# The MLP of an attention, convolution-gate and mixing kernel in five blocks of 924 tokens and one pass over its weights

## The chip, the cores and the metric

One core of a Trainium2 chip runs the whole program. The metric is device time in microseconds (us) from launch to end. Three runs of the kernel before took 1380.43 to 1383.66 us, median 1380.76.

Its engines run side by side, each through its own instructions in order: PE (TensorE) multiplies matrices into the accumulators (PSUM, eight banks of 512 floats per partition), DVE (VectorE), ACT (ScalarE) and POOL (GpSimd) work element by element, and SP (SyncE) issues the transfers between DRAM and on-chip memory.

## The reference, cut to what matters

Three stages follow each other on 8 sequences of 576 tokens (4608 in all). Only the last one, and its preparation, is touched here.

```
x  = attention(q, k, v, w_phi)                      # linear attention, 8 heads of 64
x  = (sigmoid(causal conv of x) * (x @ w_val)) @ w_out
u  = x + real(fft2(x))                              # over the sequence and the 512 features
un = (u - mean(u)) / sqrt(var(u) + 1e-6)            # over the 512 features: "LN"
y  = u + relu(un @ w_ch1) @ w_ch2                   # 512 -> 2048 -> 512: "MLP"
```

## The kernel before, in words

Every product is done in three matmuls on operands split into a high and a low part (high x high, high x low, low x high). A split is two instructions: `o_hi` (a rounding copy on ACT) and `o_lo` (a subtraction on DVE or POOL).

**The MLP's products.** Both layers use Strassen's scheme for 2x2 blocks in Winograd's form: seven products of sums of blocks instead of eight. The two halves of a block's tokens are one side of the 2x2, so a matmul is as wide as half a block. The sums of the weights' quarters are made once, in the mixing (`note_sums`, L375), and lie in DRAM (`w_scr`): eight pieces of 128 columns for each of 8 parts `j` of the 2048 hidden features, of both layers.

**Blocks and passes.** Nine blocks of `TB` = 512 tokens (L25), so matmuls of `HB` = 256 columns. The split weights of half the hidden features fill on-chip memory, so there are two passes over the blocks (`blocks`, L542): in the first, parts 0 to 3, the partial sums go to DRAM (`part_scr`) and the normed block to `un_scr`; in the second, parts 4 to 7, both come back. `prep_w` (L662) loads raw weight sums, 448 KB at a time, and splits them: three parts in the mixing's end, the others in the first block and at the turn between the passes (`note_mlp`, L1072). `prep_un` (L770) makes the seven operands out of a normed block by four subtractions and seven splits, for each of the 18 block passes.

**Units.** `c1_units` (L799) is the first layer of a pair of parts: seven products of 12 matmuls, into banks x, y and z, with copies, sums, relus and splits between them (13 or 14 DVE instructions and 14 of ACT). x has two banks, which the units take in turn. The results are the `h` tiles. `c2_units` (L874) is the second layer: seven products of 12 matmuls into cx, cy and cz, each then added to `acc`, which begins as u and leaves as the output. The second layer of a pair runs between the products of the next pair's first layer.

**LN.** `ln_stages` (L713) sums over features by DVE or POOL additions and a matmul with ones, into a bank of its own (mean). For block 0 it runs in the mixing, for the others in the MLP's first pass.

**What sets the order.** From the mixing on, all instructions are noted as operations with what they read and write, and `place_ops` (L1112) puts them in an order by planned durations and due times. It also chooses DVE or POOL for those marked "vp". On the chip each engine, and SP's queue of transfers, keeps that order, and each instruction waits for what it reads and for the place that it writes. There are stages, by which pools are open: at the mixing's end `open_last` and `open_mlp` (L564) open the tiles of the first layer, and in the last stage `open_mlp2` (L588) puts `h`, second-layer weights and `acc` where the mixing's tiles lay (among them `u`, the mixing's result on its way to DRAM).

In the profile nearly every instruction of these stages has line L62, that of the helper that issues it (L657 for transfers), so tiles tell them apart: x, y, z, cx, cy, cz are banks, un and h operands, w, wo and wg weights, A the block in LN, T scratch.

Of the kernel before, what the change touches and what calls it, by code (L numbers as in the profile page):

```python
# [20 lines left out]
NT = NB * S  # L21
# [3 lines left out]
TB = 512  # L25
HB = TB // 2
NBK = NT // TB
# [38 lines left out]
def attention_moe_mixer_kernel(  # L66
# [93 lines left out]
    un_scr = [dram.tile([128, 4, TB], F32, name=f"un_scr{t}") for t in range(NBK)]  # L160
# [3 lines left out]
    keep = pool(ctx, "keep", 1)  # L164
    wo_all = keep.tile([128, 2, 4 * DM], F32R, name="wo")
    wo = [wo_all[:, i].rearrange("p (c f) -> p c f", f=DM) for i in range(2)]
    P = {"g1": pool(ctx, "g1", 1)}

    mix = ExitStack()
# [22 lines left out]
    late["s1"] = ln_p.tile([128, TB], F32, name="s1")  # L192
    late["A"] = ln_p.tile([128, 4, TB], F32, name="A")
# [234 lines left out]
    def open_mix2():  # L428
# [3 lines left out]
        late["u"] = x2.tile([128, 4, S], F32, name="u")  # L432
        late["u256"] = x2.tile([97, S], F32, name="u256")
# [3 lines left out]
        for i in range(2):  # L437
            late["f", i] = x2.tile([128, 2, 2, NE], F32R, name=f"f{i}")
            late["Y", i] = x2.tile([128, 2, 2, NL], F32R, name=f"Y{i}")
            late["xr", i] = x2.tile([128, NE], F32R, name=f"xr{i}")  # L440
            late["rem", i] = x2.tile([128, NL], F32R, name=f"rem{i}")
            late["T0", i] = x2.tile([128, 2, HB], F32, name=f"T0{i}")
            late[("sh0", "sl0")[i]] = x2.tile([128, HB], F32R, name=("sh0", "sl0")[i])
        for i in range(4):
            late["ps", i] = ps.tile([128, 512], F32, name=f"ps{i}")
# [100 lines left out]
    NJP = NJ // 2  # L546
    NH_SLOTS = 7
    blocks = [(0, t) for t in range(NBK)] + [(1, t) for t in reversed(range(NBK))]
    wt = [[], []]
    wr = []  # L550
    un_op = []
    hs = []
    h_more = []
# [4 lines left out]
    def w_tiles(p, i, j):  # L558
        return [[p.tile([128, 7, 128], F32R, name=f"w{i}_{j}_{o}_{k}") for k in range(2)] for o in range(2)]

    def w_views(t):
        return [t[:, 896 * k:896 * k + 896].rearrange("p (q f) -> p q f", f=128) for k in range(2)]

    def open_mlp():  # L564
        p = pool(lx, "lx", 1, side=R)
        ps = pool(lx, "pss", 1, PSUM, side=R)
        late["mean"] = ps.tile([128, HB], F32, name="mean")
        for n in ("x0", "y"):
            late[n] = ps.tile([128, 2, HB], F32, name=n)
        for j in range(2):  # L570
            late["w", 0, j] = w_tiles(p, 0, j)
        for n in ("c11", "c12", "c22"):
            late[n] = p.tile([128, 2, HB], F32, name=n)
        for n in ("sh", "sl"):
            late[n] = p.tile([128, HB], F32R, name=n)
        for i in range(2):
            late["T", i] = p.tile([128, 2, HB], F32, name=f"T{i}")
            late["wr", i] = p.tile([128, 7, 128], F32, name=f"wr{i}")
# [3 lines left out]
        g = [P["g1"].tile([128, 2304], F32R, tag=f"g{i}", name=f"wg{i}") for i in range(2)]  # L582
        late["w", 0, 2] = [w_views(t) for t in g]
        late["w", 0, 3] = [w_views(wo_all[:, i]) for i in range(2)]
        h_more.extend(t[:, 1792:2304].rearrange("p (o f) -> p o f", f=HB) for t in g)
        h_more.append(wo_all[:, :, 1792:2048])

    def open_mlp2():  # L588
        big = pool(ctx, "big", 1)
        ps = pool(ctx, "psb", 1, PSUM)  # L590
        for n in ("x1", "z", "cx", "cy", "cz"):
            late[n] = ps.tile([128, 2, HB], F32, name=n)
        for i in range(NH_SLOTS):
            for k in range(2):
                late["h", i, k] = big.tile([128, 2, HB], F32R, name=f"h{i}_{k}") if 2 * i + k < 2 * NH_SLOTS - 3 else h_more.pop()
        for j in range(NJP):
            late["w", 1, j] = w_tiles(big, 1, j)
        for q in range(4):
            late["acc", q] = big.tile([128, 2, HB], F32, name=f"acc{q}")

    def late_tiles():
        for n in ("c11", "c12", "c22", "x0", "x1", "y", "z", "cx", "cy", "cz", "s1", "A", "sh", "sl", "mean", "u", "u256", "fs", ("T", 0), ("T", 1)):
            tl[n] = later(n)
        wr.extend(later(("wr", i)) for i in range(2))
        un_op.extend([later(("un", i, k)) for k in range(2)] for i in range(7))
        hs.extend([later(("h", i, k)) for k in range(2)] for i in range(NH_SLOTS))
        for i in range(2):
            for j in range(NJP):
                wt[i].append([[later(("w", i, j), o, k) for k in range(2)] for o in range(2)])
        for q in range(4):  # L610
            tl["acc", q] = later(("acc", q))

# [4 lines left out]
    BANKS = {"x0", "x1", "y", "z", "cx", "cy", "cz", "mean", "ps", "pv", "pa", "nm"}  # L617
    STAGES = {k: (a, b) for a, b, n in (
# [3 lines left out]
    ) for k in n.split()}  # L622

    def stage(k):
        n = k if isinstance(k, str) else k[0]
        if n in ("w", "ge"):
# [33 lines left out]
    wcount = [0]  # L660

    def prep_w(i, j, e):  # L662
        for o in range(2):
            b = wcount[0] % 2
            wcount[0] += 1
            h, l = wt[i][j % NJP][o]
            raw = wr[b]
            r = raw.rearrange("p q f -> p (q f)")
            wk = [("w", i, j % NJP, o, k) for k in range(2)]
            o_dma([(r, w_scr[i][j, o, :, 128:1024])], [("w_scr", i, j, o)], [("wr", b)], 448)  # L670
            was = {2: [("ge", 1, m, k) for m in range(4) for k in range(2)], 3: ["wo"]}.get(j, []) if i == 0 else []
            o_hi(h, raw, 896, [("wr", b)], [wk[0]] + was)
            o_lo(e, l, raw, h, 896, [("wr", b), wk[0]], [wk[1]] + was)
            yield
# [9 lines left out]
    AK = [("A", i, j) for i in range(2) for j in range(2)]  # L684

    def load_a(t, src):
        a = tl["A"]
        if src is un_scr:
            o_dma([(a, src[t])], [("un_scr", t)], AK, 1024)
            return  # L690
        parts = list(segments(t * TB, TB))
        o_dma([(a[:, :, o:o + n], src[b][:, :, s:s + n].rearrange("c p s -> p c s")) for o, n, b, s in parts],
              [("u_scr", b) for o, n, b, s in parts], AK, 1024)

    def load_acc(ps, t, q, after=[]):
        a = tl["acc", q]
        if ps:
            o_dma([(a, part_scr[t][q])], [("part", t, q)], [("acc", q)], 256)
            return
        i, j = divmod(q, 2)  # L700
        o_dma([(a[:, :, o:o + n], u_scr[b][2 * i:2 * i + 2, :, s:s + n].rearrange("c p s -> p c s"))
               for o, n, b, s in segments(t * TB + j * HB, HB)],
              after + [("u_scr", b) for o, n, b, s in segments(t * TB + j * HB, HB)], [("acc", q)], 256)

    def store_acc(ps, t, q):
        if ps == 0:
            o_dma([(part_scr[t][q], tl["acc", q])], [("acc", q)], [("part", t, q)], 256)
            return
        i, j = divmod(q, 2)
        o = t * TB + j * HB  # L710
        o_dma([(out[2 * i:2 * i + 2, :, o:o + HB].rearrange("c p s -> p c s"), tl["acc", q])], [("acc", q)], [], 256)

    def ln_stages(t, e1=K["ln"]):  # L713
        a, s1 = tl["A"], tl["s1"]
        nt, nh, nl = ("T0", "sh0", "sl0") if t == 0 else ("T", "sh", "sl")
        halves = [slice(0, HB), slice(HB, TB)]

        def add(o, x, y, e, r, w):
            o_tt(e, o, x, y, ALU.add, HB, r, w)

        def mean(k):
            sh, sl = later(nh), later(nl)
            b, p = ("mean", tl["mean"]) if t else next(ring)
            p = p[:, 0:HB]
            o_hi(sh, s1[:, halves[k]], HB, [("s1", k)], [nh])
            o_lo(e1, sl, s1[:, halves[k]], sh, HB, [("s1", k), nh], [nl])
# [4 lines left out]
            op("m", 0, f, [nh, nl], [b], 0.218)  # L731
            return b, p

        for k, hk in enumerate(halves):
            for c in range(1, 4):
                add(s1[:, hk], s1[:, hk] if c > 1 else a[:, 0, hk], a[:, c, hk], e1,
                    [("A", c // 2, k), ("A", 0, k), ("s1", k)], [("s1", k)])
        for k, hk in enumerate(halves):
            pk, p = mean(k)
            for c in range(2):  # L740
                b = a[:, 2 * c:2 * c + 2, hk]
                o_tt("v", b, b, p.unsqueeze(1).to_broadcast([128, 2, HB]), ALU.subtract, 2 * HB,
                     [pk, ("A", c, k)], [("A", c, k)])
        for k, hk in enumerate(halves):
            for c in range(2):
                q = later((nt, c))
                o_act(q, a[:, 2 * c:2 * c + 2, hk], ACTF.Square, 2 * HB, [("A", c, k)], [(nt, c)])
# [722 lines left out]
```

## Time and profile before

| | |
|---|---|
| runs, median of 3 | 1380.76 us |
| the profiled execution | 1378.82 us |
| its span, first to last instruction | 1377.0 us |
| PE busy | 1330.1 us (97%), 14672 matmuls |
| DVE busy | 1183.7 us (86%) |
| ACT busy | 820.5 us (60%) |
| POOL busy | 582.0 us (42%) |
| moved by transfers | 186.97 MB, mean 136 GB/s |

"Busy" is the time in which an engine has an instruction under way. Matmuls are pipelined and overlap: the record of one lasts some 280 ns, while the next starts much earlier, so their rate is read from starts. The MLP begins to run alone at about 622 us; its full rate begins at 649.8, and its last first-layer product is issued before 1361.3. A share of transfers is the part of the time in which the core's 16 DMA engines were busy, on average.

### The profile page before, as it was taken

The numbers are of one execution on the slowest core, as the hardware profiler recorded it, in microseconds if no ns is written. First come the engines' busy times: TensorE is split into PE (matmuls) and PEld (weight loads), VectorE is DVE, ScalarE is ACT, GpSimd is POOL, SyncE is SP. The second block draws the span as 40 slices with busy tenths as digits, with TensorE's granted clock in tenths as the row PEclk, the third lists the DMA queues.
The fourth block names the chain that finished last, engine by engine and source line by source line (L and its number), as shares of the span: only waits on it lengthen the run. The fifth ranks groups of instructions, "written<-read, shape, count | busy, mean of one in ns | idle before, by whom it ended". The sixth has DMA issues, their size and how long they took to land.

```text
span 1377.0 us, 35052 instructions
## 1 busy us (share of the span) xinstructions
PE 1330.1 (97%) x14672; PEld 1288.3 (94%) x14672; DVE 1183.7 (86%) x2006; ACT 820.5 (60%) x1554; POOL 582.0 (42%) x452
## 2 busy tenths in 40 slices
PE   8999999997999999996999999999999999999998
PEld 7888888887999999996999999999999999999998
DVE  7999999887889999887899999999897777777776
ACT  6888888865555546465565565555565445544542
POOL 3978888613666654342533234343223111111110
PEclk9999999998999999998999999999999999999999
DMA  7477777643444440144422333222543212222211
GB/s 266 144 278 272 272 266 263 223 159 121 144 161 161 162 146 35 66 151 167 161 85 85 119 97 123 94 77 77 177 122 105 77 62 78 93 62 92 92 47 46
DMA packets 89849, 186.97 MB, mean 136 GB/s; under 512 B 10454, under 2 KB 37334, under 8 KB 87516
## 3 DMA queue, kind: packets, MB, share of 16 engines
q1 hardware_dynamic: 85312, 174.25, 37.7%
q10 hardware_dynamic: 4380, 10.50, 2.0%
q8 instruction: 115, 1.88, 0.6%
q14 instruction: 42, 0.34, 0.1%
HBM read 121.79 MB, written 62.93 MB: 134 GB/s over the span
## 4 chain that ended last, share of the span: by engine, by line
PE 71%; DVE 21%; ACT 4%; issue 2%; DMA 1%; SPq 0%; POOL 0%; ACTq 0%; DVEq 0%
PE x L62 14%; PE cx L62 13%; PE ps L62 9%; PE cy L62 7%; PE y L62 7%; PE val L62 6%; PE cz L62 4%; DVE y L260 3%; PE z L62 3%; DVE m L257 3%; DVE acc L62 3%; PE kv L62 3%; PE pj L62 3%; PE nm L62 2%; DVE cv L126 2%
## 5 line engine op out<-in xcount | busy, mean ns | idle before, releaser
L62 PE MATMUL cx<-h,w 128*128 128x256 f32 x1260 | 172.9, 283 | 0.6 <-ACT y L62 0.6
L62 PEld LDWEIGHTS cx<-h,w 128*128 128x128 f32 x1260 | 161.1, 191 | 1.0 <-ACT y L62 0.7
L62 DVE TENSOR_TENSOR acc<-cx,acc 128x512 f32<-128x512 f32 x144 | 98.8, 686 | 34.8 <-PE cx L62 34.1
L62 POOL TENSOR_TENSOR un<-A,un 128x512 fp32r<-128x512 f32 x41 | 55.1, 1353 | 172.8 <-ACT un L62 169.2
L62 PE MATMUL val<-xh,wv 128*128 128x290 f32 x768 | 115.7, 306 | 4.7 <-DVE gs L62 2.6
L62 ACT ACTIVATE h<-z 128x512 fp32r<-128x512 f32 x108 | 64.4, 596 | 91.6 <-DVE z L62 91.1
L62 PE MATMUL x<-un,w 128*128 128x256 f32 x864 | 116.6, 285 | 0.4 <-DVE c L62 0.4
L62 PE MATMUL cy<-h,w 128*128 128x256 f32 x792 | 115.2, 282 | 1.2 <-DVE h L62 1.2
L62 PEld LDWEIGHTS val<-xh,wv 128*128 128x128 f32 x768 | 109.6, 196 | 6.6 <-DVE gs L62 3.0
L62 DVE SCALAR_TENSOR_TENSOR acc<-xf,cw,acc 128x576 f32<-128x576 f32 x128 | 105.1, 821 | 10.3 <-ACT acc L62 8.8
L62 PEld LDWEIGHTS x<-un,w 128*128 128x128 f32 x864 | 109.8, 193 | 0.7 <-DVE c L62 0.7
L62 PE MATMUL ps<-ge,wo 128*128 128x290 f32 x768 | 107.0, 297 | 0.6 <-ACT s L62 0.6
L62 PEld LDWEIGHTS cy<-h,w 128*128 128x128 f32 x792 | 105.0, 191 | 1.4 <-DVE h L62 1.4
L62 PEld LDWEIGHTS ps<-ge,wo 128*128 128x128 f32 x768 | 104.2, 189 | 0.8 <-ACT s L62 0.8
L62 POOL TENSOR_TENSOR un<-T,un 128x512 fp32r<-128x512 f32 x42 | 55.1, 1311 | 116.5 <-ACT un L62 116.5
L62 PE MATMUL kv<-vraw,ke 128*64 128x66 f32 x2560 | 94.5, 226 | 0.9 <-DVE kvT L302 0.4
L257 DVE TENSOR_REDUCE m<-pj 128x8 f32<-128x1024 f32 (+1 forms) x80 | 88.5, 1106 | 7.9 <-PE pj L62 7.9
L62 PEld LDWEIGHTS kv<-vraw,ke 128*64 128x64 f32 x2560 | 82.5, 138 | 12.0 <-ACT ke L269 1.1
L62 PE MATMUL pj<-wp,kqraw 64*128 64x128 f32 x1152 | 88.3, 291 | 4.8 <-DMA kqraw<-in_k_dram 4.4
L62 PEld LDWEIGHTS pj<-wp,kqraw 64*128 64x128 f32 x1152 | 72.7, 192 | 18.3 <-issue 18.2
L260 DVE TENSOR_TENSOR y<-pj,m 128x1024 f32<-128x1024 f32 (+1 forms) x80 | 88.5, 1107 | 0.4
L62 PE MATMUL nm<-kvT,qe 128*64 128x65 f32 x2304 | 83.3, 224 | 4.4 <-DVE xs L339 3.3
(200 smaller groups left out, 3515.1 us busy)
## 6 DMA issues: line engine op xcount, KB each, us to landing
raw<-in_w_ch_dram SPq DMA_DIRECT2D x16, 1024.0 KB, 5.8
wr<-w_scr SPq DMA_DIRECT2D x32, 448.0 KB, 3.5
vraw<-in_v_dram SPq DMA_DIRECT2D x16, 660.0 KB, 8.9
x_scr<-xT SPq DMA_DIRECT2D x32, 288.0 KB, 4.1
xf<-x_scr SPq DMA_DIRECT2D x8, 1152.0 KB, 6.5
u_scr<-u ACTq DMA_DIRECT2D x8, 1152.0 KB, 5.7
out_dram<-acc SPq DMA_DIRECT2D x36, 256.0 KB, 2.2
kqraw<-in_k_dram SPq DMA_DIRECT2D x15, 576.0 KB, 6.0
```

What stands on the lines that cost most here:

```text
L62: return lambda *a, **k: f(*(resolve(x) for x in a), **{n: resolve(x) for n, x in k.items()})
L126: nc.vector.tensor_scalar(out=ex, in0=hi32, scalar1=0x7FF00000, scalar2=None, op0=ALU.bitwise_and)
L257: nc.vector.tensor_reduce(out=m, in_=pv, axis=AX.X, op=ALU.max, apply_absolute_value=True)
L260: nc.vector.tensor_tensor(out=y, in0=pv, in1=m.unsqueeze(3).to_broadcast([128, 2, 2 * n, F]), op=ALU.subtract)
```

## The change

There are five blocks, four of 924 tokens and one of 912, and a single pass over the hidden features, so a matmul has 462 (456) columns. Weights are no longer kept on chip. Each product takes its operand from a ring, of ten 2 KB slots (per partition) for the first layer and six of 4 KB for the second. In block 0 `note_weights` loads a raw piece in rows of 512 bytes, splits it and stores both halves to `s_scr` in DRAM; in the other blocks it loads the stored halves. A slot's next load is noted right after the product that reads it.

A unit of the first layer is now one part `j` (products of 6 matmuls, 40 units); the second layer goes over two parts at a time as before. The bank cz is gone: product 1 starts cy anew and every product is added to `acc`; banks cx and cy are twice as wide, and x, y, z half. LN goes by half blocks, into one bank of x instead of one of its own. The LN of block 0, now 924 tokens, is spread over the mixing and passes through `un_scr`; that of the next block is spread over the units of each block, in a tile `B`. `u` moves to the end of its pool.

```diff
-TB = 512
-HB = TB // 2
-NBK = NT // TB
+HB = 462
+BLOCKS = [(2 * HB * t, HB) for t in range(4)] + [(8 * HB, NT // 2 - 4 * HB)]
...
-    part_scr = [[dram.tile([128, 2, HB], F32, name=f"part_scr{t}_{q}") for q in range(4)] for t in range(NBK)]
+    s_scr = [[dram.tile([128, n], F32, name=f"s_scr{i}_{m}") for m in range(r)] for i, (n, r) in enumerate(((512, 7 * NJ), (1024, 7 * NJ // 2)))]
...
+    NH_SLOTS = 14
+    RING = (10, 6)
+    ORDER = ((0, 4, 5, 1, 6, 2, 3), (0, 4, 5, 2, 6, 1, 3))
...
+    def note_weights(c, n):
+        per = len(s_scr[c])
+        t, r = divmod(n, per)
...
+        if t:
+            o_dma([(flat, s_scr[c][r])], [sk], [hk, lk], (256, 512)[c])
+            return
...
+        o_dma([(lo if c == 0 else lo[:, m], w_scr[c][x, :, :, q:q + 128].rearrange("o p f -> p o f")) for m, x in enumerate(js)],
+              [("w_scr", c, x, o) for x in js for o in range(2)] + ["third"] * (c == 0 and n < RING[0]), [lk], (128, 256)[c])
+        o_hi(w[:, 0], lo, cols, [lk], [hk])
+        o_lo(K["w"], w[:, 1], lo, w[:, 0], cols, [lk, hk], [lk])
+        o_dma([(s_scr[c][r], flat)], [hk, lk], [sk], (256, 512)[c])
...
+    def ln_first(k):
...
+        yield from ln_half(tl["A"], ak, k * HB, HB, tmp, lambda: next(ring), K["ln0"])
+        o_dma([(un_scr[k], tl["A"])], ak, [("un_scr", k)], 2 * HB)
+
+    def ln_block(t):
+        t0, n = BLOCKS[t]
+
+        def bank():
+            x = f"x{xn[0] % 2}"
+            return x, tl[x]
+
+        for k in range(2):
+            tmp = [(x, tl[x]) for x in ("T", "sh", "sl")]
+            yield from ln_half(tl["B"][:, :, k * HB:k * HB + n], [("B", k, c) for c in range(2)], t0 + k * n, n, tmp, bank, K["ln"])
...
+        def product(i, k, first):
...
+            w, wk = next_weights(0)
...
+                for kt in range(2):
+                    a, b = w[:, 0, kt], w[:, 1, kt]
+                    for m, (l, v) in enumerate(((a, uh), (a, ul), (b, uh))):
+                        mm(p, l, v[:, kt], start=first and kt + m == 0, stop=kt == 1 and m == 2, skip_group_check=True)
...
+            note_weights(0, wn[0] - 1 + RING[0])
...
+    def c2_units(t, pair):
+        n = BLOCKS[t][1]
+        for i in ORDER[1]:
...
+            first = i in (0, 4, 1)
...
+            note_weights(1, wn[1] - 1 + RING[1])
...
     def note_mlp():
-        store_un(0)
         c2 = iter(())
...
+        for t in range(len(BLOCKS)):
+            ln = ln_block(t + 1) if t + 1 < len(BLOCKS) else iter(())
+            for pair in range(NJ // 2):
+                c1 = chain(*(c1_units(t, 2 * pair + g) for g in range(2)))
+                for k in range(7):
                     next(c2, None)
...
+                    next(c1)
+                    next(c1)
+                    if t == 0 and pair == 0 and k == 2:
+                        for n in range(RING[1]):
+                            note_weights(1, n)
+                        for q in range(4):
+                            load_acc(0, q)
+                    unit = 2 * pair + k // 4
+                    if k in (1, 5) and unit >= (2 if t == 0 else 1):
+                        next(ln, None)
...
+                if pair == NJ // 2 - 1 and t + 1 < len(BLOCKS):
+                    drain(ln)
+                    prep_un(t + 1)
+                c2 = c2_units(t, pair)
         drain(c2)
```

## Rows read from the trace of the kernel before

**Rows 1.** Busy us by stage: window, length, engines (x instructions), clock, transfer share, GB/s.

```profile
350.00:600.00 250.00, 248.43 (x1868) 246.40 (x1867) 222.44 (x442) 135.24 (x296) 137.34 (x161) 1.00 0.37 126
700.00:1000.00 300.00, 297.83 (x2481) 296.67 (x2480) 275.70 (x463) 171.55 (x318) 108.07 (x94) 1.00 0.32 105
1000.00:1300.00 300.00, 299.42 (x2508) 299.22 (x2507) 232.66 (x354) 154.29 (x269) 56.69 (x42) 1.00 0.28 87
622.30:649.80 27.50, 16.91 (x106) 15.61 (x105) 20.92 (x35) 16.24 (x28) 6.26 (x6) 0.75 0.53 183
```

**Rows 2.** PE's waits, 649.8 to 1361.3 us: us, times, longest; first and last of five.

```profile
PE cx L62 <- DVE acc L62: 1.8, 5, 0.4
...
PE y L62 <- DVE un L62: 0.4, 1, 0.4
```

**Rows 3.** PE in order of time: start, us, operation, shape, count.

```profile
591.14 13.04 PE L62 MATMUL ps<-ge,wo 128*128 128x290 f32 x96
604.01 0.96 PE L62 MATMUL ps<-sq,Y 128*128 128x290 f32 x6
...
675.60 1.60 PE L62 MATMUL x<-un,w 128*128 128x256 f32 x12
...
682.79 1.60 PE L62 MATMUL y<-un,w 128*128 128x256 f32 x12
```

**Rows 4.** PE's longest wait between 622.3 and 649.8 us.

```profile
PE mean L62 <- ACT sh L62: 7.6, 1, 7.6
```

**Rows 5.** ACT in order of time, 629 to 640 us; in brackets idle time before, and releaser.

```profile
635.99 0.95 ACT L62 ACTIVATE w<-wr 128x896 fp32r<-128x896 f32 x1 [5.12 <-DMA u_scr<-u]
```

**Rows 6.** SP's transfers (packets, MB, share): 732.5:738, 714.5:716.8, 1370:1377, 700:715; slices of 630:640.

```profile
q1 hardware_dynamic: 544, 0.26, 18.4%
q1 hardware_dynamic: 144, 0.26, 30.1%
q1 hardware_dynamic: 816, 0.79, 32.6%
q1 hardware_dynamic: 144, 1.05, 17.0%
DMA  0362849999999999999999999999999960005336
```

**Rows 7.** Busy us in the attention, the stretch with the highest transfer share.

```profile
200.00:250.00 50.00, 48.40 (x1043) 43.05 (x1040) 47.37 (x82) 42.11 (x82) 44.43 (x18) 1.00 0.80 274
```

**Rows 8.** Transfers by kind: count, KB each, median us from issue to landing.

```profile
ws<-w_scr SPq DMA_DIRECT2D x32, 256.0 KB, 2.7
vraw<-in_v_dram SPq DMA_DIRECT2D x16, 660.0 KB, 8.9
```

**Rows 9.** SP in order of time: start and us of an issue.

```profile
674.05 0.32 SPq L657 DMA_DIRECT2D part_scr<-acc  x1
974.91 0.43 SPq L657 DMA_DIRECT2D acc<-u_scr  x1
```

**Rows 10.** Groups, 649.8 to 1361.3 us: shapes and count, busy us, mean ns of one.

```profile
L62 DVE TENSOR_TENSOR acc<-cx,acc 128x512 f32<-128x512 f32 x140 | 96.0, 686 | 31.9 <-PE cx L62 31.3
L62 DVE RECIPROCAL s<-s 128x128 f32<-128x128 f32 x30 | 27.7, 936 | 0.6 <-ACT s L62 0.6
L62 DVE TENSOR_TENSOR s<-T 128x256 f32<-128x256 f32 x14 | 5.8, 415 | 0.0
L62 POOL TENSOR_TENSOR s<-s,T 128x256 f32<-128x256 f32 x21 | 15.6, 742 | 25.5 <-DVE s L62 23.5 <-ACT T L62 1.5
L62 ACT ACTIVATE c<-z 128x512 f32<-128x512 f32 x69 | 41.1, 595 | 15.6 <-DVE h L62 11.6 <-DVE wo L62 4.0
```

**Rows 11.** PE's last products in order of time, first and last of seven.

```profile
1361.34 1.60 PE L62 MATMUL cx<-h,w 128*128 128x256 f32 x12
...
1371.41 1.66 PE L62 MATMUL cx<-wg,w 128*128 128x256 f32 x12 [0.88 <-DVE acc L62]
```

More of the change, by code (lines that the diff above doesn't have):

```diff
@@ L566, in open_mlp @@
         ps = pool(lx, "pss", 1, PSUM, side=R)
[L567 to L571, printed above, removed]
-        for n in ("c11", "c12", "c22"):
[L573 to L578, printed above, removed]
+        for n in ("x0", "y", "z"):
+            late[n] = ps.tile([128, 512], F32, name=n)
+        for i in range(RING[0]):
+            late["r0", i] = p.tile([128, 2, 2, 128], F32R, name=f"r0_{i}")
+        for n in ("c11", "c12", "c22"):
+            late[n] = p.tile([128, HB], F32, name=n)
         for i in range(7):
@@ L705, in store_acc, with from_u @@
[L705 to L708, printed above, removed]
-        i, j = divmod(q, 2)
[L710 to L726, printed above, removed]
+    def from_u(a, t0, n, q=slice(0, 4), after=[], w=[]):
+        parts = list(segments(t0, n))
+        o_dma([(a[:, :, o:o + m], u_scr[b][q, :, s:s + m].rearrange("c p s -> p c s")) for o, m, b, s in parts],
+              after + [("u_scr", b) for o, m, b, s in parts], w, 0.5 * n * (q.stop - q.start))
@@ L730, in f @@
                 mm(p, ones, sl, start=False, stop=True)
-            op("m", 0, f, [nh, nl], [b], 0.218)
+            op("m", 0, f, [hk, lk], [b], 2 * (n / 2400 + 0.0133))
             return b, p
[L734 to L747, printed above, removed]
-                if c:
-                    add(s1[:, hk], s1[:, hk], q[:, 0], e1, [("s1", k), (nt, c)], [("s1", k)])
-                    add(s1[:, hk], s1[:, hk], q[:, 1], e1, [("s1", k), (nt, c)], [("s1", k)])
-                else:
-                    add(s1[:, hk], q[:, 0], q[:, 1], e1, [(nt, c)], [("s1", k)])
@@ new lines, in ln_half @@
+        add(a[:, 0], a[:, 1], [ak[0]])
+        add(s1, a[:, 2], [ak[1], "s1"])
+        add(s1, a[:, 3], [ak[1], "s1"])
+        split()
+        yield
+        b, p = mean()
+        for c in range(2):
+            x = a[:, 2 * c:2 * c + 2]
+            o_tt("v", x, x, p.unsqueeze(1).to_broadcast([128, 2, n]), ALU.subtract, 2 * n, [b, ak[c]], [ak[c]])
+        for c in range(2):
+            o_act(q, a[:, 2 * c:2 * c + 2], ACTF.Square, 2 * n, [ak[c]], [tk])
+            if c:
+                add(s1, q[:, 0], ["s1", tk])
+                add(s1, q[:, 1], ["s1", tk])
+            else:
+                add(q[:, 0], q[:, 1], [tk])
@@ new lines, in ln_half @@
+        split()
+        yield
+        b, p = mean()
+        o_act(s1, p, ACTF.Sqrt, n, [b], ["s1"], bias=eps)
+        for z in range(0, n, 116):
+            x = s1[:, z:min(n, z + 116)]
+            op("v", 0, lambda e, x=x: vec.reciprocal(out=x, in_=x), ["s1"], ["s1"], 0.83)
+        for c in range(2):
+            x = a[:, 2 * c:2 * c + 2]
+            o_tt("v", x, x, s1.unsqueeze(1).to_broadcast([128, 2, n]), ALU.mult, 2 * n, ["s1", ak[c]], [ak[c]])
+        yield
+    def ln_first(k):
+        ak = [("A", c) for c in range(2)]
+        tmp = [("T0", later("T0")), ("sh0", later("sh0")), ("sl0", later("sl0"))]
+        yield from ln_half(tl["A"], ak, k * HB, HB, tmp, lambda: next(ring), K["ln0"])
+        o_dma([(un_scr[k], tl["A"])], ak, [("un_scr", k)], 2 * HB)
@@ L888, in f @@
                         for m, (v, r) in enumerate(((a, h), (a, l), (b, h))):
-                            mm(p[:, o], v, r[:, n], start=first and o + n + m == 0, stop=n + m == 3, skip_group_check=True)
-            wk = [("w", 1, j % NJP, o, k) for j in js for o in range(2) for k in range(2)]
-            op("m", 0, f, wk + [("h", s, 0), ("h", s, 1)] + ([] if first else [ct]), [ct], 12 * 0.12)
-            h_free.append(s)
-            if not (c == 0 and i == 1):
-                a = tl["acc", q]
-                o_tt("v", a, p, a, ALU.add, TB, [ct, ("acc", q)], [("acc", q)])
@@ L896, in c2_units @@
-            if c == 1 and i in (1, 2, 6, 3):
-                finish(ps, t, q)
-            yield
-    def finish(ps, t, q):
-        n = blocks.index((ps, t)) + 1
-        if not (n < len(blocks) and blocks[n][1] == t):
-            store_acc(ps, t, q)
-            if n < len(blocks):
-                load_acc(*blocks[n], q)
+                            mm(p[:, o], v, r, start=first and g + m == 0, stop=g == 1 and m == 2, skip_group_check=True)
+            op("m", 0, f, wk + [("h", s, k) for s in slots for k in range(2)] + ([] if first else [ct]), [ct], 12 * (n / 2400 + 0.0133))
@@ L1056, in note_mix @@
             note_SD(b)
-            if b == 4:
-                load_a(0, u_scr)
-                ln_stages(0, K["ln0"])
+            for k in range((b > 0) + (b == 3)):
+                next(ln0, None)
+        drain(ln0)
         b = NB - 2
-        drain(prep_w(0, 0, K["w0"]))
-        drain(prep_w(0, 1, K["w0"]))
+        for n in range(RING[0]):
+            note_weights(0, n)
+        load_first()
         note_FD(b)
```

305 lines of the change are left out of this document (130 added, 175 removed), and 4 rows, old and new, of the table STAGES.

## The prediction
> **What bounds the kernel now.** I read the 40 slices first, then busy time by stage, then what TensorE (PE) waits for, then the start times of its matmuls. After attention PE is busy nearly all the time: 248.4 of 250 us in the mixing, 297.8 of 300 in the MLP's first pass, 299.4 in its second [rows 1]. In the whole MLP from 649.8 to 1361.3 us PE's waits add up to 4.6 us [rows 2]. VectorE (DVE) reaches 275.7 of 300 us in the first pass and PE still hardly waits [rows 1], so the MLP is bound by the rate at which matmuls follow each other. That rate is read from starts, not from "busy": five groups of 12 matmuls of 256 columns start 7.19 us apart from first to last, 119.8 ns per matmul; 96 of 290 columns take 12.87 us, 134.1 ns [rows 3]. The clock is 1.00, the 2.4 GHz level, where 256 columns are 106.7 ns and 290 are 120.8. What is left, 13.1 and 13.3 ns, is paid per matmul and hardly depends on its width.
>
> **Fewer, wider matmuls.** Before: 18 block passes x 2 pairs x 7 products x 24 matmuls = 6048 of 256 columns. After: 5 blocks x 8 units x 7 products x 6, and the same number in the second layer, 3360 of 462 columns (456 in the last block; mean 460.8). The columns are the same, 1,548,288. Gone are 2688 matmuls x 13.2 ns = 35.5 us. By the straight line through the two rows instead (0.4206 ns per column) a matmul of 460.8 columns takes 205.9 ns, and 6048 x 119.8 - 3360 x 205.9 = 32.8 us. I take -34, ends -32 and -36. Nothing wider than 290 columns runs before, so the far end is nothing gained, if the extra grew with the width; the two rows speak against it. The Trainium skill ("TensorE: Matmul & The Clock Gate", section "Wait — 56ns, not 53.3ns?") puts the extra at about 2.5 ns per matmul. By it the gain would be 2688 x 2.5 = 6.7 us; the trace differs by 10 ns at both widths, so I go by the trace.
>
> **Into the MLP.** From 622.3 to 649.8 us PE has 106 instructions, 12.7 us at 119.8 ns, in 27.5 us, and its clock falls to 0.75 after the idle time: 14.8 us lost [rows 1]. The largest wait is 7.6 us, for ACT's sh [rows 4]. ScalarE (ACT) itself stands 5.12 us in front of a weight split that writes where tile u lay, until u has gone to DRAM, and everything behind it on ACT, sh among it, waits too [rows 5]. After the change u lies last in its pool, under tiles that are written later, so this wait goes. What is late next: the first two units run with no second-layer products between them. A unit's product 4 then waits for the readers of bank y: about five DVE steps of 0.63 and three ACT steps of 0.56 [rows 10], some 5 us, beside two products of 1.24 us, and DVE still ends the mixing until 629 us. I leave 8 us lost: -7, ends 0 (other waits of the same length) and -13.
>
> **Block 0: splitting while streaming.** This is the one place where a resource gets full. PE needs 672 x 205.9 ns = 138 us per block. In block 0 each weight is loaded raw, split and stored split. The transfers, by the share of 16 engines in windows that hold little else, less the 16 small packets that end each transfer [rows 6]: two transfers in 512-byte rows are 512 packets in 0.184 x 5.5 us x 16 = 16.2 us, 31.6 ns each; 1 KB takes 0.326 x 7 x 16 / 768 = 47.5 ns; 2 KB takes 0.301 x 2.3 x 16 / 128 = 86.5 ns; 8 KB rows go at 39.8 ns per KB. So a raw first-layer load (256 packets of 512 bytes) is 256 x 31.6 / 16 = 0.51 us of all engines, a second-layer one 1.01, the stores (2 KB and 4 KB rows) 0.69 and about 1.35. The sum: 46 x 0.51 + 28 x 1.01 + 56 x 0.69 + 28 x 1.35 = 128 us, with 15 for the LN input, residual and output (5.7 MB), and 15 for the first split weights that block 1 loads back: 158 us, of which the last 15 may come late. Beside 138 of PE that is full transfer engines from end to end. Over a stretch of 50 us the trace shows at most a share of 0.80 [rows 7]; in stretches of some 6 us the slices stand at 9 [rows 6]. I take 158 us for the block, +20. The ends: 141 us if everything but the last loads runs beside PE (+3), and 158 / 0.80 = 197 us (+59). The price is paid on PE at once: a split that waits for a late load holds up the ACT queue, where the copies of the first layer stand behind it. SyncE's queue has about 226 transfers to issue at 0.32 to 0.43 us [rows 9], 72 to 97 of 138 us; in it a store that waits for its split holds up the loads behind. The Trainium skill ("DMA: Bandwidth & Descriptors", section "Specifications") gives 512 bytes as enough for line rate. By it the raw loads would take 0.35 and 0.69 us and the block's transfers 142 us, 4 over PE; here 512 bytes cost 31.6 ns where a quarter of the 2 KB price is 21.6, so I go by the row.
>
> The arithmetic of the split is covered. DVE takes 0.686 us for 512 columns and 0.415 for 256 [rows 10], so some 0.63 for 462 and 1.11 for 924. A unit is 13 such steps and 3.5 additions of 924, 12.1 of 17.3 us, and LN about 16 us per block: 81%, under the 92% of the first pass now. The weights' subtractions (74 of 256 and 512 columns) are 37 us on DVE, or twice that on POOL (0.74 for 256 columns), which has 108 of 300 busy [rows 1, 10].
>
> **Blocks 1 to 4: streaming.** Each loads 28.7 MB of split weights: 56 x 0.69 + 28 x 1.35 + 15 = 92 us of 138, a share of 0.66, below the 0.80 that the attention lives with [rows 7]. The rings hold ten first-layer and six second-layer operands, about 25 us ahead; a 256 KB load lands in about 2.7 us and a 660 KB one in 8.9 at high load [rows 8]. Cost nothing; if a load came later than 25 us after its slot was free PE would wait, and only block 0 can bring that.
>
> **LN and operand preparation.** LN's two means no longer have a bank: each takes the x bank of the next unit, so that unit's first product also waits for two DVE steps of 1.11 us or a root. There are 16 means in blocks 0 to 3, each beside products of 2.5 us. The LN of 924 tokens instead of 512 in the mixing adds some 12 us to a DVE that is busy 222 of 250 us there [rows 1]. I take +4 for both; ends -2 (all the PE idle time of the first pass, as LN is spread over more of the MLP) and +16 (1 us per mean). Eighteen preparations of 512 tokens become five of 924, half the work, and the partial sums and normed blocks no longer go to DRAM and back: 0, since PE waited only 4.6 us in all [rows 2].
>
> **Tail.** The last of the seven closing products starts at 1371.41, 1.4 us later than 6 x 1.44 us after 1361.34, since it waits for an addition in its bank [rows 11]. Wider products leave 2.5 us between users of a bank; the last addition and store are 0.4 and some tenths longer: -1.
>
> **Sum.** 1378.8 (span 1377.0 and 1.8 around it) - 34 - 7 + 20 + 4 - 1 = 1360.8 us. The median of the runs stands 1.9 above the profiled execution: 1363 us.
>
> **Rivals.** (A) The forecast, block 0 partly bound by transfers: 1363, own range 1350 to 1376. Chance 0.41. (B) Transfers run beside PE throughout, block 0 costs 3: 1346. For it: the slices of 9 [rows 6], and two rings that let loads run ahead. Against it: 158 us of work in 138. Chance 0.27. The skill's rule on 512 bytes ends here, at about 1347. (C) Slower: block 0 is paced by transfers at no more than a share of 0.80, 197 us: 1363 + 39 = 1402. For it: the 0.80, and queues that run in order, as ACT's 5.12 us before a transfer shows [rows 5]; against it: the stage with 0.80 did not ask for more. It decides from a loss of 38 us in block 0, that is a block of 176 us. Chance 0.27. (D) The change doesn't do what its wider matmuls promise: the extra grows with the width and the 34 us are not there: 1397. Against it: both rows of 13 ns. Chance 0.05, the case of an extra of 2.5 ns included, which would give 1390 and is the skill's rule on matmuls.
>
> **How the numbers follow.** A measurement of this kernel can tell about 0.3%, 4.1 us, from no change. Faster by more (below 1376.6): B, and 0.36 of A: 0.63. Within: the rest of A and the near edge of C: 0.09. Slower: C's rest and D: 0.28. The range goes from a little below B, 1341, to C, 1402, which leaves about a tenth outside on either side.
>
> **What would show it.** Matmuls of 462 columns starting 205 to 206 ns apart confirm the first step; 216 would be D. Block 0's length between the first and the second block's first products against the other four, with the DMA share in it and PE's waits there (for weights or for ACT and DVE behind them), decides between A, B and C. Between the mixing and the first full group of products no wait for u's transfer should be left. PE waits on x before a unit's first product would show the shared bank. Blocks 1 to 3 of much more than 138 us would make the prediction wrong in a place where I allow nothing.

## The result, and the profile after

The changed kernel takes 1396.70 us, median of 4 runs (1394.83 to 1397.84), beside 1381.08 for the kernel before (four runs by then): a ratio of 1.0108, 95% interval 1.0091 to 1.0126. It is slower by 1.1%; I had forecast 1363 and faster. The profiled execution took 1397.84 us with a span of 1396.0, 19.0 more than the span before.

Busy time by stage of the changed kernel: window, length, then PE, its weight loads, DVE, ACT and POOL (with instructions), PE's granted clock, share of the transfer engines, GB/s.

```profile
350.00:600.00 250.00, 245.79 (x1829) 242.55 (x1828) 224.97 (x430) 134.87 (x288) 149.17 (x172) 0.99 0.38 129
600.00:649.00 49.00, 38.62 (x232) 35.99 (x230) 31.73 (x50) 21.01 (x50) 18.02 (x11) 0.90 0.29 98
649.00:677.00 28.00, 0.00 (x0) 0.00 (x0) 3.92 (x7) 2.62 (x7) 4.38 (x5) 0.53 0.97 319
677.00:820.00 143.00, 136.20 (x623) 121.02 (x624) 118.45 (x169) 97.72 (x197) 75.37 (x74) 0.96 0.89 299
820.00:960.00 140.00, 140.00 (x667) 125.36 (x666) 110.41 (x156) 71.49 (x128) 37.66 (x26) 1.00 0.77 247
960.00:1100.00 140.00, 140.00 (x666) 125.17 (x666) 110.83 (x156) 70.52 (x127) 35.46 (x25) 1.00 0.77 245
1100.00:1240.00 140.00, 140.00 (x668) 125.43 (x668) 111.42 (x156) 70.22 (x127) 33.66 (x24) 1.00 0.76 245
1240.00:1380.00 140.00, 139.88 (x673) 125.97 (x672) 97.74 (x143) 60.74 (x113) 2.70 (x2) 1.00 0.69 217
```

The third row is new: 28 us in which PE executes nothing while the transfer engines are full. The row above it belongs to it: 49 us in which those engines are used at only 0.29. From 820 us on PE has no gap, as in the MLP before [rows 1]. PE's longest waits, whole span (us, times, longest):

```profile
PE x L61 <- ACT c L61: 28.2, 1, 28.2
PE ps L61 <- ACT x2b L61: 6.8, 2, 6.4
PE y L61 <- DVE h L61: 6.6, 2, 6.1
...
PE ps L61 <- DVE fs L61: 3.5, 1, 3.5
```

The name in the first row, a copy on ACT, is not the cause. ACT and DVE in order of time, with idle time before an instruction and its releaser in brackets, lead further back, to two loads:

```profile
673.18 0.42 ACT L61 ACTIVATE r<-r 128x256 fp32r<-128x256 f32 x1 [23.99 <-DMA r<-w_scr]
```

```profile
664.30 0.64 DVE L61 TENSOR_TENSOR s<-B 128x462 f32<-128x462 f32 x1 [17.17 <-DMA B<-u_scr]
```

ACT stands 24 us before a weight split whose raw load isn't there, with the copies of the first units behind it. DVE stands 17 us before the LN of the next block. What SyncE's queue did in that time (start, us, transfer, count):

```profile
595.72 4.14 SPq L637 DMA_DIRECT2D r<-w_scr  x6
599.92 0.46 SPq L637 DMA_DIRECT2D un_scr<-A  x1
604.69 0.81 SPq L637 DMA_DIRECT2D un<-un_scr  x2
638.77 1.96 SPq L637 DMA_DIRECT2D r<-w_scr  x4
...
656.23 0.47 SPq L637 DMA_DIRECT2D s_scr<-r  x1
...
662.48 5.32 SPq L637 DMA_DIRECT2D s_scr<-r  x6
668.29 0.40 SPq L637 DMA_DIRECT2D r<-w_scr  x1
```

and what it waited for, 595 to 690 us, with PE's last matmuls on the mixing's table `ft`:

```profile
SPq L637 <- PE ps L61: 33.7, 2, 33.4
SPq L637 <- DMA u_scr<-u: 9.9, 2, 7.1
```

```profile
637.24 1.61 PE L61 MATMUL ps<-ft,f 128*128 128x258 f32 x12
```

For 33.4 us the head of the queue is one load: the first second-layer weights, whose tile lies where tiles of the mixing were. It goes at 638.77, while the last of these twelve matmuls is under way; the mixing's other products run on until 643.9. Behind it stand the ten stores of first-layer weights split long before and the refills that follow them in the ring. The queue then stands once more, for 7.1 us until 652.24, before a load of the accumulators: part of `u` isn't in DRAM yet. After that everything that was held up, and the accumulators and the next block's residual too, comes at once; the first refill is issued at 668.29. I shall call 600 to 690 us the hand-over.

The pitch of the matmuls, from starts in order of time:

```profile
1001.04 2.69 PE L61 MATMUL x<-un,r 128*128 128x462 f32 x12
1003.57 2.68 PE L61 MATMUL cx<-h,r 128*128 128x462 f32 x12
```

Twelve of 462 columns take 2.53 us, 211 ns each; from 820 to 1240 us 1997 matmuls start, 210.3 ns apart (the rows by stage have 2001, since a matmul at the edge of two windows is in both). Before, 256 columns took 119.8 and 290 took 134.1 [rows 3].

### The profile page after: what moved, and what is told of

Read it like the earlier page. It is cut to its first block, busy times and chain, and to the rows that moved or that the text cites. A ratio compares the mean times of both kernels' runs of the same rounds, so it can differ in the third digit from the quotient of the medians.

```text
span 1396.0 us, 30247 instructions
## 1 busy us (share of the span) xinstructions
PE 1315.1 (94%) x11952; PEld 1199.8 (86%) x11952; DVE 1125.7 (81%) x1794; ACT 799.7 (57%) x1540; POOL 590.2 (42%) x454
## 4 chain that ended last, share of the span: by engine, by line
PE 70%; DVE 16%; DMA 5%; ACT 4%; issue 2%; POOL 1%; SPq 1%; ACTq 0%; POOLq 0%; DVEq 0%
PE x L61 14%; PE cx L61 14%; PE cy L61 11%; PE y L61 7%; PE ps L61 6%; PE kv L61 4%; PE z L61 3%; DVE acc L61 3%; PE val L61 3%; PE pj L61 3%; PE nm L61 3%; DVE y L258 2%; PE yt L308 2%; DMA r<-w_scr 2%; DVE m L255 2%
## 5 line engine op out<-in xcount | busy, mean ns | idle before, releaser
L61 PE MATMUL x<-un,r 128*128 128x462 f32 (+1 forms) x960 | 226.0, 374 | 28.2 <-ACT c L61 28.2
L61 PEld LDWEIGHTS x<-un,r 128*128 128x128 f32 x960 | 181.6, 189 | 49.7 <-ACT c L61 28.6
L61 PE MATMUL cx<-h,r 128*128 128x462 f32 (+1 forms) x960 | 214.2, 371 | 0.1
L61 PEld LDWEIGHTS cx<-h,r 128*128 128x128 f32 x960 | 180.4, 188 | 21.0 <-DVE h L61 0.5
L61 PE MATMUL cy<-h,r 128*128 128x462 f32 (+1 forms) x720 | 162.0, 374 | 0.0
L61 PEld LDWEIGHTS cy<-h,r 128*128 128x128 f32 x720 | 136.9, 190 | 15.8
L61 PE MATMUL y<-un,r 128*128 128x462 f32 (+1 forms) x480 | 116.3, 378 | 6.6 <-DVE h L61 6.6
L61 PEld LDWEIGHTS y<-un,r 128*128 128x128 f32 x480 | 91.9, 192 | 18.0 <-DVE h L61 7.4
L61 DVE TENSOR_TENSOR acc<-cx,acc 128x924 f32<-128x924 f32 (+1 forms) x80 | 88.7, 1109 | 14.2 <-PE cx L61 8.1
L61 DVE TENSOR_TENSOR acc<-cy,acc 128x924 f32<-128x924 f32 (+1 forms) x60 | 66.8, 1113 | 39.0 <-PE cy L61 38.5
```

Source lines behind the costliest of these rows:

```text
L61: return lambda *a, **k: f(*(resolve(x) for x in a), **{n: resolve(x) for n, x in k.items()})
```

## The experiments

**The order of the hand-over (three kernels).** The planner that writes out the queues doesn't know that two tiles lie in the same place; it can be told by a key that one step writes and the other reads. No dependency of the program changes, only the plan: the places in the queues and, since the planner also chooses between DVE and POOL, the engine of some steps. e2 moved none; in e1 and e3 DVE has 13 steps more than in the changed kernel (1807 beside 1794 instructions) and POOL 13 fewer.

```diff
 # e1: on the last batch's final matmuls, and on what overlies their tiles
-op("m", 0, prod, yk, [k], (8 - a) * 0.134)
+op("m", 0, prod, yk, [k] + ["mixed"] * (b == NB - 1), (8 - a) * 0.134)   # the products with ft likewise
-  ... ["third"] * (c == 0 and n < RING[0]), [lk], (128, 256)[c])
+  ... ["third"] * (c == 0 and n < RING[0]) + ["mixed"] * (c == 1 and n < RING[1]), [lk], (128, 256)[c])
-load_acc(0, q)
+load_acc(0, q, ["mixed"])
-from_u(a, t0, n, w=ak)                                # the next block's residual
+from_u(a, t0, n, after=[("u_scr", NB - 1)] * (t0 == 2 * HB or t0 == 3 * HB), w=ak)
 # e2: the store of LN's second half goes ahead of the loads that wait for attention's tiles
-  ... + ["third"] * (c == 0 and n < RING[0])
+  ... + ["third", ("un_scr", 1)] * (c == 0 and n < RING[0])   # load_first() likewise
```

> Planned order only: the first second-layer weight loads, the load of the accumulators and of the second block's residual are planned behind the last matmuls of the mixing, whose tiles they lie over, so that on SyncE's queue the stores of split weights and the first-layer refills stand ahead of them. Theory Q (a transfer that waits for the mixing's end holds up SyncE's whole queue from 605 to 639 us, and the 28.2 us that PE stands at 649 to 677 follow from it): the stand goes to under 8 us and the time falls by 20 to 28 us, to 1369-1377 us. Rival T (the transfers' volume paces the hand-over and block 0; the order only says which of them is late): PE loses the same 25 us or more, there or in the course of block 0, 1391-1400 us. Rival W (the loss lies in the per-matmul cost, the hand-over is hidden by something else): also within 5 us of the changed kernel.

> Planned order only: the store of the second half of the normed block and its two waiting readers' loads are planned ahead of the weight loads and the other normed halves, which wait for the attention's tiles. In the changed kernel this store is issued 16 us after its data are there, and PE waits 6.4 and 3.5 us in the mixing behind it. Theory Q: these two waits go, the mixing ends some 6 to 12 us sooner, and the long stand of 28.2 us is left, or grows a little since it ends with a weight load that waits for the mixing's last matmuls: 1386-1392 us. Rival T (transfers' volume): no change, 1394-1399 us.

> Both orders of planning together. Theory Q: the gains add, 26 to 38 us below the changed kernel, 1359-1371 us, which is faster than the kernel before (1381). Rival T: 1388-1400 us, transfers stay the limit wherever they are put.

Measured: e1 1375.81 us (ratio to before 0.9957, 0.9941 to 0.9972), e2 1382.75 (1.0009, 0.9995 to 1.0023), e3, both, 1367.39 (0.9899, 0.9883 to 0.9915). Against the changed kernel these are 21, 14 and 29 us less. Theory Q's numbers hold for e1 and e3, rival T's and W's don't. In e1 the stores run while the mixing goes on, and the long stand is 6.0 us; the wait for x2b is left:

```profile
609.32 15.05 SPq L637 DMA_DIRECT2D s_scr<-r  x7
```

```profile
PE x L61 <- ACT c L61: 8.6, 3, 6.0
PE ps L61 <- ACT x2b L61: 6.6, 2, 5.7
```

e1 moves three kinds of loads at once, the weights, the accumulators and the residual; what each of them is worth alone was not tried. e2 gave more than I expected: its PE waits are

```profile
PE x L61 <- ACT c L61: 23.5, 1, 23.5
PE y L61 <- DVE h L61: 7.1, 2, 6.4
PE ps L61 <- DVE fs L61: 3.4, 1, 3.4
PE ps L61 <- POOL f L61: 2.2, 3, 1.0
PE ps L61 <- ACT x2b L61: 0.9, 1, 0.9
```

The 6.8 us for x2b are 0.9, and the long stand too is 5 us shorter; the 3.5 for fs, which I had also put down to this store, stayed. These waits are 10.6 of the 14 us; the rest is not traced. In e3 SyncE's queue runs through the hand-over, stores and refills by turns:

```profile
590.86 6.88 SPq L637 DMA_DIRECT2D r<-w_scr  x10
597.99 15.83 SPq L637 DMA_DIRECT2D s_scr<-r  x7
613.92 0.39 SPq L637 DMA_DIRECT2D r<-w_scr  x1
614.37 0.50 SPq L637 DMA_DIRECT2D s_scr<-r  x1
```

and after 640 us these of PE's waits are left:

```profile
PE x L61 <- ACT c L61: 8.4, 3, 5.9
PE y L61 <- DVE h L61: 5.1, 1, 5.1
PE cx L61 <- DVE acc L61: 0.6, 1, 0.6
```

So the 1.1% loss is an order, not the price of streaming: with the order mended the same change is faster than the kernel before by 1.0%.

The wait of 5.1 us is no transfer's. It ends at 773.9 us, where block 0 passes into block 1 (the changed kernel has it too, 6.1 us at 805.3), and DVE works through it:

```profile
772.19 1.11 DVE L61 TENSOR_TENSOR un<-A,un 128x924 fp32r<-128x924 f32 x1
773.23 0.63 DVE L61 TENSOR_TENSOR h<-y,h 128x462 fp32r<-128x462 f32 x1
```

The second step frees bank y for PE. Ahead of it the plan put the end of block 1's LN and the first of its operands; in the changed kernel DVE has no idle time at all from 795 to 805.3 us, and PE works 4.2 of these 10.3.

**The price of a matmul by width (two kernels).**

```diff
+for n in WIDTHS:
+    for r in range(8):
+        for i in range(6):
+            nc.tensor.matmul(bank[r % 2][:, 0:n], wt[:, i], mv[:, i % 2, 0:n], start=i == 0, stop=i == 5)
```

> No part of the computation, the output is zeros: groups of six f32r matmuls, each with its own 128x128 weights, into two banks by turns; twelve widths from 128 to 512 columns with no transfers and no other engine at work, then 256, 462, 256, 462, 512 and 290 columns beside a stream of 256 KB loads, then 256 and 462 columns while VectorE and ScalarE read another bank. Theory G (the extra grows with the width by itself): at 2.4 GHz 13 ns above columns / 2.4 GHz at 256 and 290, 17 to 18 ns at 462, in all three parts. Rival X (a fixed extra of 13 ns per matmul, the rest is contention): 205-206 ns at 462 without transfers and 209-211 ns beside transfers or beside the other engines' reads. Rival F (an extra that belongs to this kernel alone): neither; at 462 under 200 ns.

> No part of the computation, the output is zeros: the pitch of f32r matmuls by width again, with no transfers beside them: 256 to 304 and 376 to 512 columns in steps of 8. Theory hump: the extra above columns / 2.4 GHz is 13 to 14 ns up to 384 columns and near 512, and rises to 15-20 ns between about 400 and 496, so that 512 columns cost less per column than any width between. Rival alignment: the extra depends on whether the width is a multiple of 16, 32 or 64 columns, so that neighbours in steps of 8 jump by 3 ns or more.

e4's stretches (columns as in the rows by stage; a window also counts the matmul or two that began before it): 462 columns beside transfers, 512 beside transfers, 462 beside DVE and ACT.

```profile
186.00:216.00 30.00, 30.00 (x143) 26.75 (x142) 0.00 (x0) 0.00 (x0) 0.00 (x0) 1.00 1.05 384
...
264.00:296.00 32.00, 32.00 (x143) 26.49 (x142) 0.00 (x0) 0.00 (x0) 0.00 (x0) 1.00 0.84 307
...
335.00:358.00 23.00, 23.00 (x110) 20.51 (x110) 11.52 (x18) 10.30 (x19) 0.00 (x0) 1.00 0.00 1
```

Worked out from first and last start of each stretch of 48 or 144, in ns per matmul; "extra" is above columns / 2.4 GHz, the mean where both kernels have the width:

```
columns          256    290    384    416    448    456    462    464    480    488    512
e4, alone      120.3  133.6  173.4  188.3  206.6      -  211.6      -  216.9      -  226.9
e4, transfers  120.0  136.6      -      -      -      -  211.7      -      -      -  226.8
e4, DVE + ACT  119.9      -      -      -      -      -  211.7      -      -      -      -
e8, alone      120.0      -  173.5  186.6  202.8  208.8  211.5  208.8  216.9  225.7  227.2
extra (alone)   13.5   12.7   13.4     14     18   18.8   19.1   15.5   16.9   22.3   13.7
```

Transfers at 384 GB/s and two engines reading another bank change nothing at 256 and 462 columns (at 290, transfers cost 3 ns): rival X falls, and F. Theory G has its number at 462, but as "grows with the width" it falls too: 512 columns pay the 13.5 ns of 384. Between some 430 and 510 columns the extra is 15 to 22 ns, and neighbours 8 columns apart differ by up to 6 (480, 488), so both the hump and the alignment that I had put against each other are partly there; but 448 columns differ by 4 ns between the two kernels (206.6 and 202.8), each a single run. No simple rule came out; what stays is that 462 columns alone are 5 ns dearer than my straight line through 256 and 290 has them (206.4). In the kernel they take 210.3, 1.3 less than alone; why is open. Every matmul here loads weights of its own, and what part of the extra that is was not tried.

**What block 0's transfers cost (three kernels).** All from the reordered kernel e3.

```diff
 # e5: six blocks of 768 tokens
-HB = 462
-BLOCKS = [(2 * HB * t, HB) for t in range(4)] + [(8 * HB, NT // 2 - 4 * HB)]
+HB = 384
+BLOCKS = [(2 * HB * t, HB) for t in range(5)] + [(10 * HB, NT // 2 - 5 * HB)]
 # e6: raw weights in rows of 1 KB
-w_scr = [dram.tile([NJ, 2, 128, 8 * 128], F32, ...
+w_scr = [dram.tile([NJ, 128, 8, 2, 128], F32, ...
 # e7: no stores of split weights
-o_dma([(flat, s_scr[c][r])], [sk], [hk, lk], (256, 512)[c])
+o_dma([(flat, w_scr[c][r % NJ, 0][:, 0:(512, 1024)[c]])], ...
-o_dma([(s_scr[c][r], flat)], [hk, lk], [sk], (256, 512)[c])
```

> The reordered kernel (both orders of planning) with six blocks of 768 tokens, so matmuls of 384 columns in place of 462 and 456. By the pitches measured alone (173.4 ns at 384 columns) 4032 matmuls take 699 us; the 3360 of 462 and 456 columns take 704 us by their starts in the changed kernel: 5 us less. PE has 116.5 us of work in a block then, and block 0's transfers stay as they are. Theory H (the pitch at 462 columns is an expensive one, and transfers cost block 0 little more than the 8 us that PE stands there): 1360-1366 us. Rival T (transfers pace block 0): block 0 stays as long as with 924 tokens, so of the 22 us that its matmuls are shorter most are lost: 1375-1390 us. Before: 1381.

> The reordered kernel with the raw weights laid out in DRAM so that block 0 loads them in rows of 1 KB instead of 512 bytes; the writers before it, in attention and mixing, get rows of 512 bytes instead of 2 KB. By the packet times read before the change (31.6 ns for 512 bytes, 47.5 for 1 KB) a raw first-layer load takes 0.38 us of all engines instead of 0.51 and a second-layer one 0.76 instead of 1.01: 13 us of transfer time less in block 0. Theory T (what is left of block 0's loss, some 10 us, is the transfers' rate): 4 to 10 us faster than the reordered kernel, 1357-1363 us. Rival H (it is the order of waits at the hand-over, not the rate): 1365-1369 us. If the writers' smaller rows slow attention, 1370 us or more, seen before 600 us.

> The reordered kernel without the stores of the split weights in block 0; blocks 1 to 4 load as many bytes in the same rows from the unsplit weights instead, so the output is not the reference's. This takes 84 transfers and, by the packet times, 56 x 0.69 + 28 x 1.35 = 76 us of transfer time out of block 0, half of what stands there. Theory T (transfers' rate): block 0's share falls from 0.96 to about 0.6 and PE's losses after 650 us go: 8 to 12 us faster, 1355-1360 us. Rival H (hand-over order): the waits of 5.9 us and 1.8 us near 640 us stay, 1364-1369 us.

Measured: e5 1375.84 (0.9954, 0.9936 to 0.9972), e6 1370.22 (0.9915, 0.9894 to 0.9937), e7 1363.14 (0.9862, 0.9831 to 0.9893). e5 lies in rival T's range, e6 just above H's (1369), e7 between T's and H's. 640 to 820 us, block 0 with its lead-in, in e3 and then in e7:

```profile
640.00:820.00 180.00, 169.34 (x775) 149.78 (x776) 147.39 (x215) 113.55 (x224) 71.38 (x69) 0.96 0.95 320
```

```profile
640.00:820.00 180.00, 170.29 (x792) 150.57 (x792) 148.49 (x216) 114.56 (x227) 83.28 (x78) 0.97 0.59 185
```

Without the stores the share falls from 0.95 to 0.59, about as the packet times said, but PE gains 1 us of busy time, and the median is 4 lower, with intervals that overlap: a price of some 0 to 10 us. Of e7's waits

```profile
PE x L61 <- ACT c L61: 6.9, 2, 5.9
PE cy L61 <- DVE h L61: 2.8, 1, 2.8
```

the first two, 5.9 and 1.0 us, are those near 640 that rival H wanted left; the third stands at 774 us in place of e3's 5.1, under a plan with six steps fewer on DVE. e6's smaller transfer times gave nothing: 1370.22 is 3 above e3 (the intervals overlap), where theory T wanted 4 to 10 less. Its profiled execution is only 1 us behind e3's at 610 us, so slower writers ahead of the mixing's end, the third case that I had named, explain little of it. So at 924 tokens block 0's transfers fit almost entirely beside PE. At 768 they don't: e5's matmuls run at the pitch measured alone (12 in 2.08 us, 173 ns),

```profile
899.89 2.24 PE L61 MATMUL cx<-h,r 128*128 128x384 f32 x12
901.97 1.20 PE L61 MATMUL y<-un,r 128*128 128x384 f32 x6
```

and between 749 and 811 us, where block 0 passes into block 1, PE waits for split weights, which it does nowhere in e3:

```profile
PE z L61 <- DMA r<-s_scr: 4.1, 1, 4.1
PE x L61 <- DMA r<-s_scr: 3.4, 3, 1.6
```

The transfer engines stand at 0.94 to 0.96 there and still at 0.91 from 820 to 960 us. Of the two sizes tried, 924 tokens lie on the good side.

**Width and the last u (four kernels).** e9 is e3 with HB = 464, e12 the changed kernel with HB = 464; e10 and e11 make the following edit at 464 and at 462.

```diff
-o_tt(K["uf"], u[:, cs, 0:HS + 1], ...                # the next line alike
+o_tt("v" if b == NB - 1 else K["uf"], u[:, cs, 0:HS + 1], ...
-... [("u_scr", b)], 1152, K["su"])
+... [("u_scr", b)], 1152, "d" if b == NB - 1 else K["su"])
```

> The reordered kernel with one number changed: blocks of 928 tokens in place of 924, matmuls of 464 columns (and 448 in the last block) in place of 462 (and 456). By the pitches measured alone (208.8, 202.8 against 211.5, 208.6 ns) 2688 and 672 matmuls take 697.5 us in place of 708.7: 11 us less. Theory P (the price of a matmul depends on its exact width, and PE's rate is what bounds blocks 1 to 4): 1355-1360 us, with matmuls of 464 columns starting 207 to 209 ns apart. Rival S (the pitch alone doesn't carry over, in the kernel 462 columns took 210 and not 211.5): a gain of 0 to 5 us, 1362-1368 us.

> Blocks of 928, and the last batch's u is added on VectorE alone and stored from SyncE's queue in place of ScalarE's, so that ScalarE's copies for the first units stand behind neither GpSimd's addition nor the store. Theory Q (a queue's head holds up what stands behind it, here 4.85 and 1.6 us on ScalarE, seen as PE's wait of 5.9 us): 2 to 5 us faster than blocks of 928 alone. Rival: the first units' wait is VectorE's own work at the mixing's end, which now has 2 us more: 0 to 2 us slower.

> The reordered kernel with blocks of 924 and, as the one difference, the last batch's u added on VectorE and stored from SyncE's queue. With blocks of 928 this edit went with 7 us less, though its profile shows only 2.1. Theory Q (the edit itself is worth about 7 us): 1358-1363 us. Rival (blocks of 928 and the edit give something together, the edit alone gives what the profile shows): 1363-1368 us.

> The changed kernel with blocks of 928 tokens in place of 924 and nothing else, its order of transfers as it was. Theory P (five microseconds of matmul pitch, seen as 208.6 against 209.6 ns in the reordered kernel): 1390-1393 us. Rival S (the pitch's gain is lost elsewhere or too small for the spread of runs): 1394-1399 us.

Measured: e9 1367.77 (0.9906, 0.9891 to 0.9921), e10 1360.77 (0.9846, 0.9832 to 0.9861), e11 1360.25 (0.9856, 0.9834 to 0.9878), e12 1389.36 (1.0070, 1.0048 to 1.0091). 464 columns take some 209 ns in the kernel beside 210.3. From one block's first product to the next one's it is 142.2 us beside 143.0 in the profiles, and the last block, of 448 columns, is 2.8 us shorter: worth some 6 us in all, if every block gains alike. The times show a gain once in three pairs (e12 beside the changed kernel, 7 us, whose intervals just touch; not e9 beside e3, nor e10 beside e11). In the profiles e12's gain has another 3.8 us in it, the wait for DVE's h (2.8 beside 6.6), and e9 and e10 come to the mixing's last output products 3.2 and 4.1 us later than e3 and e11, before any of these matmuls. So the gain in pitch is there, and the times don't separate it. The edit on the last u went with 7 us less at both widths, but not by the mechanism that I named: ACT still stands 5.13 us before the same piece of u in e11 (4.85 in e3), only for DVE instead of GpSimd. What shrank are PE's waits after 635 us, from the 14.1 us above in e3 to 9.0 in e11, these 8.5 and two small ones:

```profile
PE x L61 <- ACT c L61: 5.2, 1, 5.2
...
PE cy L61 <- DVE h L61: 2.1, 1, 2.1
PE cy L61 <- DVE acc L61: 1.2, 1, 1.2
```

The largest part is e3's wait of 5.1 us at 774 us, where the first block ends, 130 us behind the edit. There the plan is another: in e11 the step `un<-A,un` no longer stands ahead of `h<-y,h`, and besides the edit's own step six steps went from DVE to POOL and one came back. So the 7 us can't be put down to the edit by itself; a kernel with the edit and e3's plan elsewhere was not tried. e10 and e11 beat both kernels, by 1.4 to 1.5% the one before.

## Why the prediction was wrong, point by point

In spans the account is 19.0 = -21 (pitch) + 32 (orders, 1396.0 - 1364.0 of e3; 29 by the medians) + 8 (all the rest). I had -34 and +16. The measured time lies inside my range of 1341 to 1402 only because the range reached to rival C, whose mechanism it wasn't: that is luck.

- **"Into the MLP", -7: the step that failed.** I wrote that with u last in its pool the wait before the split goes, and left 8 us. That wait did go from ACT, but I asked only which tile lies over u, not which load overlies the mixing's own tiles and where it stands in SyncE's queue. I had named such a queue ("a store that waits for its split holds up the loads behind") and applied it inside block 0 alone. The 28.2 us stand replaced 14.8 us lost before [rows 1, 4]. e1 shows it: 21 us.
- **"LN and operand preparation", +4: too small, and for another reason.** No wait for LN's use of the x bank is on PE's list. e2 shows 14 us from a store 16 us late in the same queue, part of it in the mixing, part in the stand behind it. And the making of block 1's operands costs 5 to 6 us at the end of block 0, where DVE is full.
- **"Fewer, wider matmuls", -34: the far end was nearer than I allowed.** 2688 x 210.3 + 672 x 207.3 (the last block's starts) = 704.6 against 724.6, -20; with the 120.2 ns that the kernel before takes over 820 to 1240 us, -22: I take -21. Two points 34 columns apart could not carry a line to 462; e4 has 19.1 ns extra there alone and 13.4 at 384. Rival D's mechanism was half there. The Trainium skill ("TensorE: Matmul & The Clock Gate", section "Wait — 56ns, not 53.3ns?") has a fixed extra of some 2.5 ns; for these matmuls no width shows less than 10, and it isn't fixed.
- **"Block 0", +20: mis-sized.** The work was estimated well: a share of 0.95 over 180 us in e3 is 171 us of full engines, against my 158 with less of the lead-in. But I took 0.80 [rows 7] for something like a ceiling, and it was only what that stage asked for; full engines hide beside PE at a cost of some 0 to 10 us (e7). Rival B was right in this term. Rival C forecast the right sign by a mechanism that the runs refute: with the order mended its 39 us are not there. The sign that I had set, from a block's first product to the next block's, would have misled: it is 172.6 us for block 0 (154.7, 143.1 and 143.0 for the next three), close to C's 176, but the stand of 28.2 us lies in it; in e3 it is 157.0.
- **"Blocks 1 to 4", nothing: right.** PE is busy 420.00 of 420 us from 820 to 1240, at a share of 0.77 where I had 0.66. The share had no consequence, but why it is higher was not looked into. **DVE covered**: right as a mean, 110 to 111 of 140 us (79%; forecast 81%), and wrong at the end of block 0, where PE waits for a full DVE.
- **The check that I set** for the hand-over, "no wait for u's transfer should be left", fails as it stands: SyncE's queue waits 7.1 us for it. It was also too narrow: it looked for the old wait, not for any.

## What to carry to other kernels

When a change lays new tiles over old ones, list for every queue the first transfer that must wait for the old tiles' last reader, and what stands behind it: a queue that runs in order turns one early-planned load into a stop for transfers that were ready. A planner that doesn't know of overlaid storage should be told by an explicit key; here a few such keys were worth 29 us and turned the sign. The planner makes a new plan after every edit, so look for what else moved before putting a gain down to the edit. Don't extend a cost per instruction to a size that the trace doesn't show without measuring it, and don't read the highest share a stage reaches as what the engines can give.

## What the runs showed of the hardware

- The price of an fp32r matmul with weights of its own above columns / 2.4 GHz, alone, is 10 to 14 ns from 256 to 304 columns, 13.4 at 384 and 13.5 at 512, and 15 to 22 between 430 and 510 (e4, e8). Transfers beside it change nothing at 256, 462 and 512 columns and add 3 ns at 290; DVE and ACT on another bank change nothing at 256 and 462. 456 and 464 columns take the same 208.8 ns, 376 and 384 the same 173.4.
- The transfer engines held 0.95 of their time over 180 us (320 GB/s) beside a PE that lost 10.7 us of 180 (e3); with loads in 2 KB rows alone they moved 384 GB/s (e4).
- After idle stretches PE's clock stands at its lower level, 1.2 GHz, and the first products pay: six matmuls of 462 columns took 2.68 us after the stand of 28 us in the changed kernel (granted clock 0.52 from 677.2 to 681.8 us), and as much after only 5.09 us in e3 (0.50 from 773.9 to 776.4), in place of 1.43:

```profile
773.91 2.68 PE L61 MATMUL y<-un,r 128*128 128x462 f32 x6 [5.09 <-DVE h L61]
```
